# Two chunks share each feed-forward product behind a recurrence, with fewer gate banks, more sum banks and output stores by batch

## The chip, the cores and the metric

The kernel runs on one core of a Trainium2 chip. The metric is the device time of one execution in microseconds. The engines are TensorE (PE in the profile, with its weight loads as PEld), VectorE (DVE), ScalarE (ACT), GpSimd (POOL) and SyncE (SP, which here only issues transfers and reads a flag).

## The reference

An attention-like recurrence over 768 steps (4 batches, 8 heads of 40), then two gated feed-forward layers on the 3072 tokens of 320 features, each with 1536 hidden features:

```python
for t in range(S):
    y[:, :, t] = einsum('bhd,bhde->bhe', r_t, state)
    Sa = einsum('bhde,bhe->bhd', state, a_t)
    state = state * w_t[:, :, None, :] - einsum('bhd,bhe->bhde', Sa, b_t) + einsum('bhd,bhe->bhde', v_t, k_t)
x = y.transpose(0, 2, 1, 3).reshape(3072, 320)
x = (silu(x @ w_gate) * (x @ w_val)) @ w_out          # moe
x = (sigmoid(x @ w2_gate) * (x @ w2_val)) @ w2_out    # moe2
```

## The kernel before

The tokens are cut into 12 chunks of 256. Every f32 product is made from two-part splits: an upper part in fp32r and the rest, with three products for each pair. So a hidden block `f` (128 of the 1536 features, 12 blocks) of a chunk takes 16 matmuls of 256 columns for gate and value (`Ffn.gate`, line 1109: eight each; `w[..]` weights stationary, the chunk's `x` moving), a silu or sigmoid on ScalarE (1113), a multiply on VectorE (1114), the split of the product into `hh` (ScalarE, 1115) and `hl` (GpSimd, 1116), and 6 matmuls of 320 columns that add the block to two sums `po0`, `po1` (`Ffn.add`, 1125). The adds of block `f` come behind the products of block `f+1`.

The first part of the program (`attention`, called from line 1348) makes the recurrence chunk by chunk and weaves into it the weight decode of layer 1 and layer-1 blocks of chunks that are ready (there gate and value share one bank, `gv`). How many blocks each chunk got there stands in `used`: 3, 5, 5, 5, 5, 5, 5, 5, 5, 7, 10 and 12. All of its feeds `x` are kept in DRAM (`xd`), the partial sums in `xs`.

The second part, from line 1351 on, is the stream (`Ffn.stream`, 1143): a list of jobs, one for each chunk and layer. The 11 chunks with layer-1 blocks left come first (72 blocks), then layer 2 for all 12 chunks (144 blocks): 216 chunk-steps of 16 products and 6 adds. Layer-1 jobs load `x` from `xd` (`load_x`), and their sums are added to `part` on VectorE (`end1`, 1401) and stored. Layer-2 jobs load that result, transpose and split it (`split_x`, `split_steps`, 1055), and copy their two sums on ScalarE and VectorE (`end2`, 1409), then store them (1410), each as one transfer of 2 x 64 x 320, since the two halves of the 128 partitions belong to two batches. Gate and value have two banks each (`g0`, `g1`, pool `b_pg` with 2 buffers).

Layer-2 weights come as pairs of 32-bit words of 64-bit floats and are decoded in 36 steps of 384 or 320 columns (`load_w`, three steps for each of 12 blocks). A step is: absolute value into `dt` on ScalarE (1005); clamp on GpSimd (1008); shift (1011) and merge (1012) on VectorE; sign and exponent into `ds` (1016, 1017) on VectorE; upper part `w` on ScalarE (1027); rest on GpSimd (1029) and its sum with `ds` into `w` (1031 and 1033, or 1035). In the stream the work tiles `dt` and `ds` come from two places in turn (`m_tmp` and `at_static`), and two weight buffers (`m_wb`) are spare, so that decoding starts before layer-1 weights come free. `each1` calls up to three decode steps a layer-1 job, then all that are left.

A scheduler sets the order of instructions on each engine from these calls and from the tiles they wait for; within an engine that order is then fixed. Behind the stream, line 1446 reads a flag and 1447 branches over a fallback that doesn't run on these inputs:

```python
ok = nc.values_load(fl[0:1, 0:1], min_val=0, max_val=1)
with tc.If(ok < 1):
```

Of the kernel before, what the change touches and what calls it, by code (L numbers as in the profile page):

```python
# [18 lines left out]
P = 128  # L19
# [5 lines left out]
FEW = 3  # L25
NWB = 2
DM = H * D
# [8 lines left out]
def raw_of(pool, tags=RAW):  # L36
    return [(pool, t) for t in tags]
# [940 lines left out]
class Ffn:  # L978
# [64 lines left out]

    def split_steps(self, xs):

        nc = self.nc
        x = self.new_x()
        lo, hi = slice(0, 64), slice(64, 128)
# [80 lines left out]
    def ffn(self, x, ws, silu, tag):  # L1129
# [11 lines left out]
        self.used = f  # L1141

    def stream(self, jobs):

        pend = None
        get = jobs[0][3]
        for j, (ws, silu, tag, _, each, end) in enumerate(jobs):  # L1150
            for x in get:
                pass
            get = iter(()) if j + 1 == len(jobs) else jobs[j + 1][3]
            ops = self.sums(tag)
            for f, w in enumerate(ws):
                h = self.gate(x, w, silu)
                if pend is not None:
                    pend()
                last = f == len(ws) - 1

                def pend(ops=ops, w=w, h=h, f=f, last=last, end=end):
                    self.add(ops, w, h, f == 0, last)
                    if last:
                        end(ops)

                each(f)
                if f >= len(ws) - 4 and (nx := next(get, None)) is not None:
                    get = iter((nx,))
        pend()
# [116 lines left out]
def rwkv_moe_kernel(ctx, tc, r, k, v, w, a, b, aw0, aw, aa, akb, av, avt, art, w1a, w2a, out):  # L1286
# [11 lines left out]
    with ExitStack() as c1:  # L1298
# [52 lines left out]
        with ExitStack() as c2:  # L1351
            pool2 = lambda n, b, **kw: c2.enter_context(tc.tile_pool(name=n, bufs=b, **kw))
            wb = pool2("m_wb", NWB)
            y_p, x_q = pool2("m_y", 2), pool2("m_xq", 1)
            pt, pg, po = pool2("b_tp", 2, space=PSUM), pool2("b_pg", 2, space=PSUM), pool2("b_po", 1, space=PSUM)

            tmp = pool2("m_tmp", 1)
            raws = [[t, *raw_of((st, tmp)[i % 2])[1:]] for i, t in enumerate(three)]
            ffn = Ffn(nc, ident, (raws, x_p, h_p, pt, pg, po), False)
            slots = [(wb, "w8")] * NWB + [(st, t) for t in spare_tags] + first + [(st, t) for t in tags]  # L1360

# [4 lines left out]

            ahead = load_w2()

            left = [blk for blk in range(NB) if used[blk] < NF]

            def load_x(blk):
                ffn.x = (x_q, x_p)[left.index(blk) % 2]
                x = ffn.new_x()
                nc.sync.dma_start(out=x.bitcast(F32), in_=xd[blk])
                yield x

            def split_x(blk):
                xin = y_p.tile([P, 2, DM + 64], F32, tag="xin", name="xin")
                src = xs[1][2 * blk : 2 * blk + 2].rearrange("u p e -> p u e")
                nc.sync.dma_start(out=xin[:, :, 0:DM], in_=src)  # L1380
                nc.sync.dma_start(out=xin[:, :, DM:], in_=src[:, :, 256:DM])
                yield
                ffn.x = (x_q, x_p)[(len(left) + blk) % 2]
                yield from ffn.split_steps([xin[:, 0], xin[:, 1]])

            parts = {}

            def each1(blk, f):
                if f == 0:
# [8 lines left out]
            def end1(blk, ops):  # L1398
# [7 lines left out]
            def end2(blk, ops):  # L1406
# [5 lines left out]
            def check(blk, f):  # L1412

                if f in (2, 6, 10):
# [23 lines left out]
            flag, jobs, seen = [], [], []  # L1438
            for blk in left:
                jobs.append((w1[used[blk] :], True, "po", load_x(blk), partial(each1, blk), partial(end1, blk)))  # L1440
            for blk in range(NB):
                jobs.append((w2, False, "po", split_x(blk), partial(check, blk), partial(end2, blk)))
            ffn.stream(jobs)
# [54 lines left out]
```

## Time and profile before

| | us |
|---|---|
| median of 3 runs | 1301.01 (1299.7 to 1302.88) |
| the profiled execution, own time | 1302.28 |
| its span in the trace | 1300.6 |
| TensorE, VectorE, ScalarE, GpSimd busy | 1204.2, 710.7, 600.4, 561.7 |
| 0 to 600: TensorE busy | 524.9 |
| 600 to 675: TensorE busy | 67.3 |
| 675 to 850: TensorE busy | 174.3 |
| 850 to 1288.5: TensorE busy | 437.7 |
| 1288.5 to 1300.6: TensorE busy | 0.0 |

The lower rows cut the span by what is done: recurrence, its last chunk with layer-1 blocks, the stream while the second layer's weights are decoded, the stream after that, and what follows TensorE's last matmul. Matmuls overlap in the records (a `g` of 256 columns has a mean duration of 282 ns), so the time that one takes is read from the starts of neighbours, not from that mean. The granted clock is TensorE's, as a share of 2.4 GHz; its mean over the span is 0.948.

### The profile page before, as it was taken

To read this page: it belongs to the slowest core of one execution; us is meant where nothing else is said; L and a number is where in the kernel's file an instruction comes from. 1 tells how busy PE (TensorE), PEld (TensorE's weight loads), DVE (VectorE), ACT (ScalarE), POOL (GpSimd) and SP (SyncE) were. 2 spreads that over 40 slices of the span, in tenths; PEclk is the share of its full clock that TensorE was granted. 3 is DMA by queue.
4 is the path that set the end of the run, shared out by engine and by line. 5 is a ranking of instruction groups with operands and counts; after the bars stand their busy time and mean duration, and the time that the engine had idled before them with its cause. 6 is when DMAs were issued, how large, how long until landed. Compare 5 with 4: busy or idle time off the path is not lost.

```text
span 1300.6 us, 34364 instructions
## 1 busy us (share of the span) xinstructions
PE 1204.2 (93%) x14209; PEld 1158.9 (89%) x14209; DVE 710.7 (55%) x1432; ACT 600.4 (46%) x1447; POOL 561.7 (43%) x749
## 2 busy tenths in 40 slices
PE   5477989999999999899989999999999999999996
PEld 4466878889889998898889999999999999999996
DVE  6858558876788667966889877322111212121121
ACT  8354555656655665455434444323333333333331
POOL 5767143323223324357867898422222222222221
PEclk8677767999999999999999999999999999999998
DMA  7445534545644554333555544211000000000000
GB/s 216 128 126 150 157 113 116 132 95 130 158 112 107 112 145 119 93 102 112 177 181 162 179 140 143 88 63 42 11 23 23 24 23 23 24 23 23 11 11 14
DMA packets 179750, 124.56 MB, mean 96 GB/s; under 512 B 133888, under 2 KB 159488, under 8 KB 178816
## 3 DMA queue, kind: packets, MB, share of 16 engines
q1 hardware_dynamic: 179584, 122.27, 34.1%
q8 instruction: 113, 1.85, 0.6%
q14 instruction: 53, 0.43, 0.1%
HBM read 90.81 MB, written 31.43 MB: 94 GB/s over the span
## 4 chain that ended last, share of the span: by engine, by line
PE 59%; DVE 19%; ACT 8%; issue 5%; DMA 4%; POOL 3%; SPq 0%; POOLq 0%; ACTq 0%; DVEq 0%
PE g L1109 32%; PE po L1125 16%; DVE pr L525 4%; PE gv L1109 2%; DVE part L531 2%; PE kps L485 2%; PE aps L858 1%; PE tp L370 1%; DVE lq L497 1%; DMA wt<-in_a_w_dram 1%; ACT bn L495 1%; DVE g L1114 1%; DVE am L867 1%; DVE part L822 1%; ACT bn L494 1%
## 5 line engine op out<-in xcount | busy, mean ns | idle before, releaser
L1109 PE MATMUL g<-x,w 128*128 128x256 f32 x3456 | 478.6, 282 | 3.3 <-DVE g L1114 2.6
L1109 PEld LDWEIGHTS g<-x,w 128*128 128x128 f32 x3456 | 449.7, 190 | 4.0 <-DVE g L1114 3.1
L1116 POOL TENSOR_TENSOR hl<-g,hh 128x256 fp32r<-128x256 f32 x288 | 224.9, 782 | 462.8 <-ACT hh L1115 452.7
L1114 DVE TENSOR_TENSOR g<-g,g 128x256 f32<-128x256 f32 x216 | 91.2, 423 | 357.0 <-PE g L1109 347.2
L1115 ACT CAST hh<-g 128x256 fp32r<-128x256 f32 x288 | 116.8, 406 | 247.3 <-DVE g L1114 221.8
L1125 PE MATMUL po<-w,hh 128*128 128x320 f32 x1152 | 227.2, 311 | 1.8 <-ACT hh L1115 1.6
L1125 PEld LDWEIGHTS po<-w,hh 128*128 128x128 f32 x1152 | 176.4, 189 | 2.8 <-ACT hh L1115 2.7
L1109 PE MATMUL gv<-x,w 128*128 128x256 f32 x1152 | 167.8, 294 | 5.3 <-DVE g L1114 3.2
L1109 PEld LDWEIGHTS gv<-x,w 128*128 128x128 f32 x1152 | 149.9, 195 | 8.5 <-DVE g L1114 4.4
L1125 PE MATMUL po<-w,hl 128*128 128x320 f32 x576 | 143.5, 314 | 3.1 <-POOL hl L1116 3.0
L1113 ACT ACTIVATE g<-g 128x256 f32<-128x256 f32 x216 | 82.7, 383 | 125.9 <-PE g L1109 118.3
L1029 POOL TENSOR_TENSOR dt<-dt,w 128x384 f32<-128x384 f32 (+1 forms) x72 | 79.0, 1098 | 72.8 <-ACT w L1027 39.2
L1125 PEld LDWEIGHTS po<-w,hl 128*128 128x128 f32 x576 | 93.1, 189 | 4.9 <-POOL hl L1116 4.7
L497 DVE TENSOR_TENSOR lq<-kps,part 64x256 f32<-64x256 f32 x96 | 40.5, 422 | 77.1 <-ACT bn L495 72.0
L525 DVE TENSOR_TENSOR pr<-part,sn 128x4 f32<-128x4 f32 (+4 forms) x135 | 75.3, 558 | 3.7
L485 PE MATMUL kps<-lq,kbt 104*128 104x128 f32 x384 | 62.4, 312 | 11.5 <-DVE lq L497 8.6
L485 PEld LDWEIGHTS kps<-lq,kbt 104*128 104x128 f32 x384 | 54.5, 219 | 15.8 <-issue 4.4
L531 DVE TENSOR_REDUCE part<-pr 128x2 f32<-128x4 f32 (+4 forms) x135 | 66.6, 493 | 2.9
L1011 DVE TENSOR_SCALAR dt<-dt 128x384 int32<-128x384 int32 (+1 forms) x72 | 48.7, 677 | 30.5 <-POOL dt L1008 30.3
L1027 ACT CAST w<-dt 128x384 fp32r<-128x384 f32 (+1 forms) x72 | 35.6, 495 | 58.6 <-DVE dt L1012 57.1
L858 PE MATMUL aps<-rbd,ut 104*128 104x128 f32 x384 | 57.1, 295 | 4.6 <-DVE ysb L903 2.0
L370 PE MATMUL tp<-ident,part 128*104 128x128 f32 x288 | 46.0, 297 | 15.3 <-ACT pend L178 6.3
(182 smaller groups left out, 1650.3 us busy)
## 6 DMA issues: line engine op xcount, KB each, us to landing
raw<-in_w_dram SPq DMA_DIRECT2D x48, 384.0 KB
xd<-x SPq DMA_DIRECT2D x12, 896.0 KB
x<-xd SPq DMA_DIRECT2D x11, 896.0 KB
raw<-in_w_dram SPq DMA_DIRECT2D x24, 320.0 KB
ld<-in_a_kb_dram SPq DMA_DIRECT2D x22, 320.0 KB
ld<-rd SPq DMA_DIRECT2D x64, 80.0 KB
pn<-pd SPq DMA_DIRECT2D x32, 160.0 KB
ld<-in_a_a_dram SPq DMA_DIRECT2D x12, 320.0 KB
```

The source lines that it names most:

```text
L370: t = nc.tensor.transpose(ps[0 : x.shape[1], n, :], x, ident)
L485: nc.tensor.matmul(kps[:, n].rearrange("p h t -> p (h t)"), lhsT=kbt[0:PW, n, :], rhs=lq[m % 3][0:PW, 4 * g4 + n].rearrange("p h t -> p (h ...
L525: nc.vector.tensor_tensor(out=o, in0=xs[:, 0:kk, None, 0:n].to_broadcast([P, kk, 2, n]), in1=sn[:, None, n : n + 2, 0:n].to_broadcast([P, ...
L531: nc.vector.tensor_reduce(out=xs[:, 0:kk, n : n + 2], in_=o, axis=AX.X, op=ALU.add)
L858: nc.tensor.matmul(aps[:, n, h2], lhsT=ut[0:PW, x, 2 * h2 : 2 * h2 + 2].rearrange("p u s -> p (u s)"), rhs=rbd[0:PW, x, h2].rearrange("p b ...
L1029: sub(out=tf, in0=tf, in1=w.bitcast(F32), op=ALU.subtract)
L1109: nc.tensor.matmul(gv[n], lhsT=p, rhs=q, start=e == 0, stop=e == len(seq) - 1)
L1113: nc.scalar.activation(out=g, in_=gv[0], func=AF.Silu if silu else AF.Sigmoid)
L1114: nc.vector.tensor_tensor(out=g, in0=gv[1], in1=g, op=ALU.mult)
L1115: nc.scalar.copy(out=hh, in_=g)
L1116: self.heng.tensor_tensor(out=hl, in0=g, in1=hh.bitcast(F32), op=ALU.subtract)
L1125: self.nc.tensor.matmul(ops[u], lhsT=p[:, us], rhs=q, start=first and n == 0, stop=last and n == 2)
```

## The change

`Ffn.gates` takes the place of `Ffn.gate` in the stream. A feed tile `x` holds two chunks ([P, 2, XW]), a matmul's moving operand is [2, 256], 512 columns, and a bank holds both chunks' products ([P, 2, 256]). So gate and value have one bank each (`b_pg` with 1 buffer), and the sums have four (`po00`, `po01`, `po10`, `po11`). Jobs are pairs of chunks: (0, 1) to (8, 9) and 10 alone in layer 1, six pairs in layer 2. Where the two chunks of a job differ in `used`, the first blocks are made for one chunk alone, and the last block of the last job is made chunk by chunk. Counted by blocks, 33 pairs and 6 singles make up layer 1, 71 pairs and 2 singles layer 2. The silu, multiply, `hh` and `hl` stay one instruction for each chunk.

`m_wb` and `m_tmp` are gone: all layer-2 steps use one `dt` and one `ds`, and the last two weights go into slots of layer-1 weights (`late`). `each1` calls one decode step for each pair block, two for late weights. The feed pool has two pair buffers (`m_xq`). `end2` stores each sum in two transfers of 64 x 320, one for each batch, on ScalarE's queue for `u == 0` of the last chunk. Line numbers below 1040 shift by -1 (the decode is 1004 to 1034, its VectorE lines 1010, 1011, 1015, 1016), the stream's products are line 1163, silu 1167, multiply 1170, `hh` 1171, `hl` 1172, adds 1124.

The diff, cut to its core:

```diff
+    def gates(self, x, w, silu, act):
+        wh, wl = w
+        n = len(act)
+        cols = lambda at: x[:, act[0] : act[0] + n, at : at + 256]
+        gv = [self.pg.tile([P, 2, 256], F32, tag=f"g{k}", name=f"g{k}") for k in range(2)]
+        for k in range(2):
...
+            for e, (p, at) in enumerate(seq):
+                nc.tensor.matmul(gv[k][:, 0:n], lhsT=p, rhs=cols(at), start=e == 0, stop=e == len(seq) - 1)
...
+        for j in range(n):
+            nc.scalar.activation(out=g[j], in_=gv[0][:, j], func=AF.Silu if silu else AF.Sigmoid)
+        for j in range(n):
+            hh, hl = new("hh", F32R), new("hl", F32R)
+            nc.vector.tensor_tensor(out=g[j], in0=gv[1][:, j], in1=g[j], op=ALU.mult)
+            nc.scalar.copy(out=hh, in_=g[j])
+            self.heng.tensor_tensor(out=hl, in0=g[j], in1=hh.bitcast(F32), op=ALU.subtract)
...
     def stream(self, jobs):
...
-            ops = self.sums(tag)
-            for f, w in enumerate(ws):
-                h = self.gate(x, w, silu)
-                if pend is not None:
-                    pend()
+            ops = [self.sums(f"po{i}") for i in range(len(firsts))]
+            for f in range(min(firsts), len(ws)):
+                act = [i for i, n in enumerate(firsts) if n <= f]
                 last = f == len(ws) - 1
...
+                for part in [[i] for i in act] if last and j + 1 == len(jobs) else [act]:
+                    hs = self.gates(x, ws[f], silu, part)
+                    if pend is not None:
+                        pend()
...
-            wb = pool2("m_wb", NWB)
-            y_p, x_q = pool2("m_y", 2), pool2("m_xq", 1)
-            pt, pg, po = pool2("b_tp", 2, space=PSUM), pool2("b_pg", 2, space=PSUM), pool2("b_po", 1, space=PSUM)
-            tmp = pool2("m_tmp", 1)
-            raws = [[t, *raw_of((st, tmp)[i % 2])[1:]] for i, t in enumerate(three)]
+            y_p, x_q = pool2("m_y", 2), pool2("m_xq", 2)
+            pt, pg, po = pool2("b_tp", 2, space=PSUM), pool2("b_pg", 1, space=PSUM), pool2("b_po", 1, space=PSUM)
+            raws = [[t, *raw_of(st)[1:]] for t in three]
...
-            slots = [(wb, "w8")] * NWB + [(st, t) for t in spare_tags] + first + [(st, t) for t in tags]
+            slots = [(st, t) for t in spare_tags] + first + [(st, t) for t in tags]
...
-                if 1 <= f <= 3:
-                    next(ahead, None)
-                if blk == left[-1] and f == NF - 1 - used[blk]:
+                if i + 1 < len(blks) and used[blks[i + 1]] <= f:
+                    return
+                rest = pairs[pairs.index(blks) + 1 :]
+                for n in range(1 if len(w2) < late else 2):
+                    at = len(w2) - late + NFA
+                    if len(w2) < late or (f > at and all(used[b] > at for p in rest for b in p)):
+                        next(ahead, None)
+                if not rest and f == NF - 1:
                     for _ in ahead:
                         pass
...
                 for u in range(2):
                     (nc.scalar.copy, nc.vector.tensor_copy)[u](out=ob[:, u], in_=ops[u])
-                    nc.sync.dma_start(out=out_rows(out, 2 * blk + u), in_=ob[:, u])
+                    eng = nc.scalar if blk == NB - 1 and u == 0 else nc.sync
+                    rows = out_rows(out, 2 * blk + u)
+                    for b2 in range(2):
+                        eng.dma_start(out=rows[b2], in_=ob[64 * b2 : 64 * b2 + 64, u])
```

TensorE's order in layer 1 of the stream, before. A `g` is a bank (gate or value) of one chunk and block, `w_...` the weights of a block, `po_...` the sums; `x6` stands for six such instructions in a row:

```order
L1109 MATMUL g_9954<-x,w_9194 128x256 x7
L1125 MATMUL po_9695<-w_8527,hh 128x320 x2
L1125 MATMUL po_9696<-w_8527,hh 128x320 x2
L1109 MATMUL g_9954<-x,w_9194 128x256
L1109 MATMUL g_9955<-x,w_9194 128x256 x8
L1125 MATMUL po_9695<-w_8527,hl 128x320
L1125 MATMUL po_9696<-w_8527,hl 128x320
```

And now:

```order
L1163 MATMUL g_9896<-x,w_8485 128x512 x8
L1163 MATMUL g_9897<-x,w_8485 128x512 x8
L1124 MATMUL po_9690<-w_7833,hh 128x320 x2
L1124 MATMUL po_9691<-w_7833,hh 128x320 x2
L1124 MATMUL po_9692<-w_7833,hh 128x320 x2
L1124 MATMUL po_9693<-w_7833,hh 128x320 x2
L1124 MATMUL po_9690<-w_7833,hl 128x320
L1124 MATMUL po_9691<-w_7833,hl 128x320
L1124 MATMUL po_9692<-w_7833,hl 128x320
L1124 MATMUL po_9693<-w_7833,hl 128x320
```

Sixteen products of both chunks now stand in a row, and the twelve adds of the block before stand behind all of them, no longer between them.

VectorE in the same part of the stream, before. Lines 1011 to 1017 are one decode step, 1114 the multiply of a block:

```order
L1114 TENSOR_TENSOR g<-g_9924,g 128x256
L1011 TENSOR_SCALAR dt<-dt 128x384
L1012 SCALAR_TENSOR_TENSOR dt<-raw,dt 128x384
L1114 TENSOR_TENSOR g<-g_9955,g 128x256
L1016 TENSOR_SCALAR ds<-dt 128x384
L1017 SCALAR_TENSOR_TENSOR ds<-raw,ds 128x384
L1114 TENSOR_TENSOR g<-g_9986,g 128x256
```

And now (1010 to 1016 are the step, 1170 the multiply):

```order
L1170 TENSOR_TENSOR g<-g_10012,g 128x256 x2
L1010 TENSOR_SCALAR dt<-dt 128x320
L1011 SCALAR_TENSOR_TENSOR dt<-raw,dt 128x320
L1015 TENSOR_SCALAR ds<-dt 128x320
L1016 SCALAR_TENSOR_TENSOR ds<-raw,ds 128x320
L1170 TENSOR_TENSOR g<-g_10071,g 128x256 x2
```

The multiplies of both chunks come together, and a whole decode step lies between one pair's and the next.

TensorE where chunk 11's last layer-1 blocks (`gv`) are made. Before, no product of the stream stands among them:

```order
L1109 MATMUL gv<-x,w_7791 128x256 x9
L1125 MATMUL po_9283<-w_2028,hh 128x320 x2
L1125 MATMUL po_9284<-w_2028,hh 128x320 x2
L1109 MATMUL gv<-x,w_7791 128x256 x5
L1125 MATMUL po_9283<-w_2028,hl 128x320
L1125 MATMUL po_9284<-w_2028,hl 128x320
```

And now (line 1163 is the stream's first block, of chunk 0 alone):

```order
L1163 MATMUL g_9694<-x,w_2028 128x256 x3
L1108 MATMUL gv<-x,w_7791 128x256 x4
L1124 MATMUL po_9283<-w_2028,hh 128x320 x2
L1124 MATMUL po_9284<-w_2028,hh 128x320 x2
L1108 MATMUL gv<-x,w_7791 128x256 x3
L1124 MATMUL po_9283<-w_2028,hl 128x320
L1124 MATMUL po_9284<-w_2028,hl 128x320
L1108 MATMUL gv<-x,w_7791 128x256 x9
L1163 MATMUL g_9694<-x,w_2028 128x256 x3
```

The stream's first products now stand in small groups between those blocks.

## Rows read from the trace of the kernel before

**Rows 1.** Table by stretch: us, length, busy time (records) of each engine, granted clock, DMA.

```profile
700.00:750.00 50.00, 49.50 (x393) 49.30 (x392) 41.67 (x68) 22.96 (x59) 43.68 (x57) 1.00 0.53 177
1000.00:1250.00 250.00, 250.00 (x1988) 249.97 (x1988) 49.72 (x113) 82.68 (x212) 69.20 (x102) 1.00 0.07 20
```

**Rows 2.** Page, costliest groups: gate products of the stream; busy, mean ns of one, idle before.

```profile
L1109 PE MATMUL g<-x,w 128*128 128x256 f32 x3456 | 478.6, 282 | 3.3 <-DVE g L1114 2.6
```

**Rows 3.** Timeline of two steps, layer 2: start us, us, engine, instruction, [idle before <-releaser].

```profile
1200.29 0.38 ACT L1113 ACTIVATE g<-g 128x256 f32<-128x256 f32 x1 [0.66 <-PE g L1109]
1200.32 1.81 PE L1109 MATMUL g<-x,w 128*128 128x256 f32 x14
1201.53 0.42 DVE L1114 TENSOR_TENSOR g<-g,g 128x256 f32<-128x256 f32 x1 [2.35 <-PE g L1109]
...
1201.97 0.74 PE L1125 MATMUL po<-w,hh 128*128 128x320 f32 x4
1201.99 0.41 ACT L1115 CAST hh<-g 128x256 fp32r<-128x256 f32 x1 [1.32 <-DVE g L1114]
...
1202.47 0.74 POOL L1116 TENSOR_TENSOR hl<-g,hh 128x256 fp32r<-128x256 f32 x1 [2.03 <-ACT hh L1115]
...
1205.85 1.81 PE L1109 MATMUL g<-x,w 128*128 128x256 f32 x14
```

**Rows 4.** Groups by form, 640 to 820 us: the decode; busy us, mean ns, idle before, releasers.

```profile
L1029 POOL TENSOR_TENSOR dt<-dt,w 128x384 f32<-128x384 f32 x24 | 28.3, 1181 | 10.7 <-DVE ds L1016 8.7 <-ACT g L1113 1.3 <-ACT dt L1005 0.6
...
L1012 DVE SCALAR_TENSOR_TENSOR dt<-raw,dt 128x384 int32<-128x384 int32 x24 | 20.9, 869 | 0.6
...
L1031 POOL TENSOR_TENSOR w<-dt,ds 128x256 fp32r<-128x256 f32 x24 | 19.3, 803 | 0.8 <-DVE ds L1017 0.8
L1011 DVE TENSOR_SCALAR dt<-dt 128x384 int32<-128x384 int32 x24 | 18.1, 752 | 2.2 <-POOL dt L1008 2.0
...
L1008 POOL TENSOR_SCALAR dt<-dt 128x384 f32<-128x384 f32 x24 | 14.6, 610 | 0.7 <-ACT dt L1005 0.7
L1033 POOL TENSOR_TENSOR w<-dt,ds 64x128 fp32r<-64x128 f32 x23 | 12.9, 563 | 0.9
L1005 ACT ACTIVATE dt<-raw 128x384 f32<-128x384 f32 x23 | 12.7, 553 | 4.5 <-POOL w L1035 3.8 <-POOL w L1033 0.7
L1027 ACT CAST w<-dt 128x384 fp32r<-128x384 f32 x24 | 12.3, 513 | 20.6 <-DVE dt L1012 20.6
```

**Rows 5.** Decode lines, whole run: engine, operation, count: shortest/median/longest ns, first and last start.

```profile
L1011 DVE TENSOR_SCALAR dt<-dt x72: 308/702/2207, 21.9 to 819.4; 128x384 int32<-128x384 int32 x48, 128x320 int32<-128x320 int32 x24
...
L1012 DVE SCALAR_TENSOR_TENSOR dt<-raw,dt x72: 475/660/1428, 22.9 to 820.3; 128x384 int32<-128x384 int32 x48, 128x320 int32<-128x320 int32 x24
...
L1029 POOL TENSOR_TENSOR dt<-dt,w x72: 857/1026/1586, 25.1 to 822.1; 128x384 f32<-128x384 f32 x48, 128x320 f32<-128x320 f32 x24
```

**Rows 6.** TensorE's timeline at the start of the stream.

```profile
675.20 4.45 PE L1109 MATMUL g<-x,w 128*128 128x256 f32 x24 [2.14 <-DVE g L1114]
679.45 0.67 PE L1125 MATMUL po<-w,hl 128*128 128x320 f32 x2
```

**Rows 7.** Timeline of the end: ScalarE's last copy and SP's last stores.

```profile
1288.40 0.42 ACT L1409 COPY ob<-po 128x320 f32<-128x320 f32 x1 [1.32 <-PE po L1125]
...
1288.85 1.12 SPq L1410 DMA_DIRECT2D out_dram<-ob  x2
```

**Rows 8.** The branch behind the stream (line 1447), as SP's queue has it.

```profile
L1447 SPq EVENT_SEMAPHORE  x8: 17/17/17, 1293.0 to 1298.8; - x8
...
L1447 SPq COMPARE_BRANCH  x1: 50/50/50, 1290.0 to 1290.0; - x1
```

**Rows 9.** Table by stretch: three microseconds: the stream's start, 128x320 stores, behind the last copies.

```profile
677.00:678.00 1.00, 1.00 (x7) 1.00 (x7) 0.42 (x1) 0.37 (x1) 1.00 (x1) 0.50 0.08 28
883.00:884.00 1.00, 0.92 (x8) 0.68 (x7) 0.20 (x1) 1.00 (x1) 0.00 (x0) 1.00 0.89 310
1291.00:1292.00 1.00, 0.00 (x0) 0.00 (x0) 0.00 (x0) 0.00 (x0) 0.00 (x0) 0.50 0.20 47
```

More of the change, by code (lines that the diff above doesn't have):

```diff
@@ L25 @@
 FEW = 3
-NWB = 2
 DM = H * D
@@ L1149, in stream @@
         get = jobs[0][3]
-        for j, (ws, silu, tag, _, each, end) in enumerate(jobs):
+        for j, (ws, silu, firsts, _, each, end) in enumerate(jobs):
             for x in get:
@@ L1153, in stream, with pend @@
             get = iter(()) if j + 1 == len(jobs) else jobs[j + 1][3]
-            ops = self.sums(tag)
-            for f, w in enumerate(ws):
-                h = self.gate(x, w, silu)
-                if pend is not None:
-                    pend()
-                last = f == len(ws) - 1
[L1161 to L1167, printed above, removed]
+            ops = [self.sums(f"po{i}") for i in range(len(firsts))]
+            for f in range(min(firsts), len(ws)):
+                act = [i for i, n in enumerate(firsts) if n <= f]
+                last = f == len(ws) - 1
+                for part in [[i] for i in act] if last and j + 1 == len(jobs) else [act]:
+                    hs = self.gates(x, ws[f], silu, part)
+                    if pend is not None:
+                        pend()
+                    def pend(ops=ops, w=ws[f], hs=hs, f=f, part=part, last=last, end=end, firsts=firsts):
+                        for i, h in zip(part, hs):
+                            self.add(ops[i], w, h, f == firsts[i], last)
+                            if last:
+                                end(i, ops[i])
+                for i in act:
+                    each(i, f)
+                if f >= len(ws) - 7 and (nx := next(get, None)) is not None:
                     get = iter((nx,))
@@ L1365, in load_w2 @@
                     w2.append(ffn.w)
-            ahead = load_w2()
+            ahead, late = load_w2(), len(spare_tags) + NFA
             left = [blk for blk in range(NB) if used[blk] < NF]
[L1371 to L1374, printed above, removed]
-                yield x
[L1377 to L1381, printed above, removed]
-                yield
-                ffn.x = (x_q, x_p)[(len(left) + blk) % 2]
-                yield from ffn.split_steps([xin[:, 0], xin[:, 1]])
+            twos = lambda xs: [xs[i : i + 2] for i in range(0, len(xs), 2)]
@@ new lines, in rwkv_moe_kernel, with new_x, load_x, split_x @@
+            pairs = twos(left)
+            def new_x():
+                return x_q.tile([P, 2, XW], F32R, tag="x", name="x")
+            def load_x(blks):
+                x = new_x()
+                for i, blk in enumerate(blks):
+                    nc.sync.dma_start(out=x[:, i].bitcast(F32), in_=xd[blk])
+                yield x
+            def split_x(blks):
+                xins = []
+                for blk in blks:
+                    xin = y_p.tile([P, 2, DM + 64], F32, tag="xin", name="xin")
+                    src = xs[1][2 * blk : 2 * blk + 2].rearrange("u p e -> p u e")
+                    nc.sync.dma_start(out=xin[:, :, 0:DM], in_=src)
+                    nc.sync.dma_start(out=xin[:, :, DM:], in_=src[:, :, 256:DM])
+                    xins.append(xin)
+                yield
+                x = new_x()
+                for i, xin in enumerate(xins):
+                    for _ in ffn.split_steps([xin[:, 0], xin[:, 1]], x[:, i]):
+                        yield
+                yield x
@@ L1386, in rwkv_moe_kernel, with each1 @@
             parts = {}
-            def each1(blk, f):
-                if f == 0:
+            def each1(blks, i, f):
+                blk = blks[i]
+                if f == used[blk]:
                     part = parts[blk] = y_p.tile([P, 2, DM], F32, tag="part", name="part")
                     nc.sync.dma_start(out=part, in_=xs[1][2 * blk : 2 * blk + 2].rearrange("u p e -> p u e"))
-                if 1 <= f <= 3:
-                    next(ahead, None)
-                if blk == left[-1] and f == NF - 1 - used[blk]:
+                if i + 1 < len(blks) and used[blks[i + 1]] <= f:
[6 more added lines that the diff above has]
+                if not rest and f == NF - 1:
@@ L1438, in rwkv_moe_kernel @@
             flag, jobs, seen = [], [], []
[L1439 to L1442, printed above, removed]
+            for blks in pairs:
+                firsts = [used[blk] for blk in blks]
+                jobs.append((w1, True, firsts, load_x(blks), partial(each1, blks), partial(end1, blks)))
+            for blks in twos(list(range(NB))):
+                jobs.append((w2, False, [0, 0][: len(blks)], split_x(blks), partial(check, blks), partial(end2, blks)))
             ffn.stream(jobs)
```

32 lines of the change are left out of this document (26 added, 6 removed).

## The prediction

> **What bounds the kernel now.** I read the table of engines by stretch first. From 1000 to 1250 us TensorE is busy all the time at granted clock 1.00, while VectorE is busy for 50 of the 250 us and GpSimd for 69 [rows 1]. So it is in nearly the whole feed-forward stream: the profile page gives its 3456 gate products 479 us of busy time and only 3.3 us of idle time ahead of them [rows 2]. There only fewer or cheaper matmuls, or what lies ahead of the first and behind the last of them, can move the end. From 700 to 750 us TensorE is as full, but there VectorE (41.7 of 50) and GpSimd (43.7) are nearly full too [rows 1]: this is where the second layer's weights are decoded, and where another order of that work can make TensorE wait.
>
> The timeline of a quiet period gives the price of a matmul. 14 gate products of 256 columns take 1.65 us from start to start (1200.32 to 1201.97), 117.9 ns each. Two steps of 16 gates and 6 adds take 5.53 us (1200.32 to 1205.85), 2.765 us each, which leaves 0.879 us for six adds, 146.5 ns for 320 columns [rows 3]. So 64 columns more cost 28.6 ns, 256 of that kind 114.4, and 3.5 ns would be left for the matmul itself. That is less than the reading tells: 10 ns in the 1.65 us move it by 11. A matmul costs its columns and next to nothing beside them.
>
> **The change, part by part.** The sum is made against the profiled execution, 1302.28 us, which is 1.27 us above the median of the runs shown; so 1.3 us go off at the end.
>
> *Paired products.* The 216 chunk-steps of 16 matmuls become 104 pairs (33 in layer 1, 71 in layer 2) and 8 singles: 3456 products of 256 columns become 1664 of 512 and 128 of 256. 1664 matmuls and as many weight loads go, and no column. The adds, 12 for a pair, stay. A product of 512 columns stands nowhere in the trace. One bound is twice 117.9, 235.8 ns, and saves nothing; a loss I exclude, as the same columns are fed with fewer weights. The other takes every gap away: 512 columns at the 2.4 GHz of clock 1.00 are 213.3 ns, 22.5 ns less, 37 us in all. I take 234.3 ns, 1.5 ns less than two, between nothing and the 3.5 ns of the line through the two sizes shown, since two points speak for that line and none for the other end: 1.5 ns by 1664 is **-2.5 us**. A pair then takes 16 x 0.2343 + 12 x 0.1465 = 5.51 us.
>
> The rows put 256 columns at 117.9 ns at clock 1.00 [rows 3]. The Trainium skill ("TensorE: Matmul & The Clock Gate", section "Back-to-back issue gap") gives a warm matmul its columns at 2.4 GHz and 2.5 ns more. That is 109.2 ns for 256 columns, which this trace does not show, and 215.8 ns for 512: by it the sum would be some 33 us lower. It is rival C.
>
> *Single gate banks.* A pair's first product into a bank must wait until ScalarE (gate) or VectorE (value) has read both chunks' halves of the pair before. Meanwhile TensorE has the other bank's eight products (1.87 us) and twelve adds (1.76 us), 3.6 us; two reads take 2 x 0.38 us on ScalarE, 2 x 0.42 on VectorE [rows 3]. Some 2.8 us are left over, so this costs nothing, unless a reader stands behind other work for that long. The decode is the work that could do it.
>
> *The decode with one work tile.* Before, consecutive decode steps had their own `dt` and `ds`, and two could overlap. Now a step's first operation (ScalarE, absolute value) waits until GpSimd has read `dt` for the step before. The loop is the sum along that chain: by the means of the busy stretch 0.553 + 0.610 + 0.752 + 0.869 + 0.513 + 1.181 + 0.803 + 0.563 = 5.84 us [rows 4], and five changes of engine, of 0.04 us (VectorE's end 1201.95 to ScalarE's 1201.99) to 0.07 us (1202.40 to GpSimd's 1202.47) [rows 3], 0.3 together: 6.1 us. With the shortest times of the three that vary most, 0.308, 0.475 and 0.857 [rows 5], it is 5.0 us. VectorE's new order is strict, two multiplies and then four decode operations, so where the loop is longer than a pair's 5.51 us it delays the multiplies pair after pair and, once the 2.8 us of cover are used, TensorE. By the order some 29 of the 36 steps lie in the stream. Bounds: nothing, and (6.1 - 5.5) x 29 = 17 us. A pair now has at most one step beside it in 5.5 us where two chunk-steps had up to one and a half, so the engines are in each other's way less, and the loop should lie between 5.0 and 5.6. I take **+2 us**.
>
> *The start of the stream.* TensorE's first stream product waits 2.14 us for VectorE, to 675.20, and the next 24 take 4.25 us (to 679.45) where 24 x 0.118 is 2.83: it had been idle, the granted clock fell to 0.50 in 677 to 678, and 1.4 us are lost [rows 6, 9]. In the changed order the first stream products stand as filler among chunk 11's last first-layer steps, as their banks are free once the recurrence is over. That fills the wait, and the low clock goes with it. Late next is chunk 11's own chain from silu to the lower half of the product, which still ends in its adds. Bounds: +2 for a wait of the old size elsewhere, -3.5 for both; I take **-2.5 us**, nearer to the removal that the order shows.
>
> *The stores by batch.* ScalarE starts the first of the two last copies at 1288.40, and SP issues the last stores from 1288.85 on, 0.56 us each [rows 7]. It branches at 1290.0, and its next event is at 1293.0, the last at 1298.8 [rows 8], 1.8 us ahead of the end of the span. For those last 5.8 us SP waits for stores. They move slowly: a share of 0.20 of the DMA engines and 47 GB/s in 1291 to 1292, where two stores of the same bytes in the form 128x320 had 0.89 and 310 GB/s in 883 to 884 [rows 9]. So it is the form 2x64x320 that is slow, and 64 x 320, with its 64 rows in front, should go like 128x320: landed well before SP's 1293.0. Late next is SP's own stretch behind the branch, 3.0 us for which the trace shows no releaser; SP has two issues ahead of the branch, as before, and ScalarE the other two, beside VectorE's copy. The end then comes some 0.4 us behind the old 1293.0 for the semaphores that are read there, and 1.9 us: 1295.3 in place of 1300.6, **-5.3 us**. Bounds 0 and -5.8. The other chunks' 22 additional stores cost SP 0.56 us each over 400 us in which nothing waits for it.
>
> *At nothing:* the splits of a pair's feed, as many as before, beside the 66 us of a job's twelve pair steps; and the two late weights, which go into layer-1 slots that come free pairs ahead of their use.
>
> Sum: 1302.28 - 2.5 + 2 - 2.5 - 5.3 = 1294.0 profiled, **1292.7 us** as a median.
>
> **The rivals.**
> *B: a matmul has a real fixed cost, and two chunks now share it.* 117.9 less 106.7 ns (256 columns at 2.4 GHz) is 11 ns; paid once, 512 columns take 225 ns and 11 x 1664 = 18 us go in place of 2.5: 1277. For it: weight loads halve in number. Against it: 320 columns show 146.5 less 133.3, 13 ns, so the excess grows with the columns.
> *C: a feed of 512 columns leaves no gap,* 213 ns: 37 us in place of 2.5, 1258. Against it: neither size shown comes near its columns' time.
> *D: slower. One work tile paces everything.* Place: the stretch of the decode, 700 to 860 us, where the multiplies stand in order behind the decode and a single bank leaves no second one to run ahead into. Price: the upper bound of above, 17 us in place of 2, 1308. It decides from a loop of 6.0 us (0.5 x 29 = 14 in place of 2, 1305). For it: the means of the stretch [rows 4]. Against it: those were made with two steps under way.
> *E: the smaller stores land no sooner,* and the end stays 12 us behind the last product: 1292.7 + 5.3 = 1298.0. For it: four stores in place of two. Against it: the rows of the 128x320 form.
>
> The Trainium skill ("DMA: Bandwidth & Descriptors", section "Rules for kernel authors") says of two transfers to disjoint halves of the partitions not to bother, since they serialize. That speaks for E; no run here shows a pair of halves.
>
> **How the numbers follow.** A measurement of this kernel tells changes of some 0.3%, 3.9 us: faster is below 1297.1, slower above 1304.9. The forecast gets 0.57, with an own range of 1286 to 1299 (the bounds of the start and the tail, and waits of up to 8 us); 0.07 of it lies within 0.3%. B gets 0.15 and C 0.04, both faster; E 0.09, within 0.3%; D 0.15, of it 0.02 within 0.3% and 0.13 slower. So faster 0.50 + 0.15 + 0.04 = 0.69, same 0.07 + 0.09 + 0.02 = 0.18, slower 0.13. The range, 1274 to 1302, takes in the forecast, B and E, and leaves out C and nearly all of D, 0.18.
>
> **What would show it.** Products of 512 columns 234 to 236 ns apart and a pair every 5.5 us (225 ns is B, 213 is C). TensorE still full at 700 to 850 us; waits on VectorE, ScalarE or GpSimd that sum to over 10 us there are D. No 2 us wait and no low clock where the stream begins. A DMA share near 0.9 for a microsecond behind the last copies, and the end of the span some 7 us behind TensorE's last product (12 is E). I am wrong if a layer-2 pair takes under 5.4 us or a layer-1 pair over 5.8 in the mean.

## The result and the profile after

| | before | changed |
|---|---|---|
| median, us (runs on one chip) | 1300.38 (1299.70 to 1302.88) | 1281.54 (1279.69 to 1282.63) |
| ratio, 95% interval | | 0.9846 (0.9831 to 0.986) |
| profiled execution, span, us | 1302.28, 1300.6 | 1282.63, 1280.9 |

The changed kernel takes 18.8 us less, where 8.3 less were forecast: the time is inside the stated range, and the gain is more than twice the one forecast. The rows of the changed kernel that answer to those of before follow. The table by stretch (columns as in [rows 1]), with one microsecond behind the last copies:

```profile
700.00:750.00 50.00, 50.00 (x263) 43.90 (x262) 29.73 (x62) 21.09 (x54) 36.04 (x49) 1.00 0.43 140
1000.00:1250.00 250.00, 250.00 (x1302) 219.07 (x1302) 44.87 (x112) 78.29 (x213) 71.08 (x104) 1.00 0.07 16
1274.00:1275.00 1.00, 0.00 (x0) 0.00 (x0) 0.00 (x0) 0.00 (x0) 0.00 (x0) 1.00 0.90 221
```

TensorE is full as before, and VectorE and GpSimd have fallen from 41.7 and 43.7 us to 29.7 and 36.0 in 700 to 750. The page's group that answers to [rows 2]:

```profile
L1163 PE MATMUL g<-x,w 128*128 128x512 f32 (+1 forms) x1792 | 419.9, 385 | 0.8 <-DVE g L1170 0.7
```

The idle time ahead of the stream's products has gone from 3.3 to 0.8 us. The timeline of a pair in layer 2 (as [rows 3]):

```profile
1199.80 3.37 PE L1163 MATMUL g<-x,w 128*128 128x512 f32 x14
...
1203.00 0.75 PE L1124 MATMUL po<-w,hh 128*128 128x320 f32 x4
```

14 products of 512 columns take 3.20 us from start to start (1199.80 to 1203.00), 228.6 ns each; I had put 234.3. TensorE's timeline from chunk 11's first layer-1 product on (as [rows 6]):

```profile
639.62 1.21 PE L1108 MATMUL gv<-x,w 128*128 128x256 f32 x8 [0.57 <-ACT x L1060]
...
665.56 0.64 PE L1163 MATMUL g<-x,w 128*128 128x256 f32 x4
...
674.94 0.85 PE L1124 MATMUL po<-w,hh 128*128 128x320 f32 x4 [0.36 <-ACT hh L1114]
675.96 0.55 PE L1124 MATMUL po<-w,hl 128*128 128x320 f32 x2 [0.17 <-POOL hl L1115]
676.38 1.20 PE L1163 MATMUL g<-x,w 128*128 128x256 f32 x8
...
678.29 1.19 PE L1163 MATMUL g<-x,w 128*128 128x256 f32 x8
...
698.84 2.08 PE L1163 MATMUL g<-x,w 128*128 128x512 f32 x8 [0.69 <-DVE g L1170]
...
707.93 3.82 PE L1163 MATMUL g<-x,w 128*128 128x512 f32 x16
...
713.35 3.82 PE L1163 MATMUL g<-x,w 128*128 128x512 f32 x16
```

The kernel before has these two waits ahead of the one in [rows 6]:

```profile
662.63 2.18 PE L1109 MATMUL gv<-x,w 128*128 128x256 f32 x16 [0.54 <-DVE g L1114]
...
672.20 0.86 PE L1125 MATMUL po<-w,hh 128*128 128x320 f32 x4 [0.91 <-ACT hh L1115]
```

The stream's products (line 1163, 256 columns) now fill the gaps among chunk 11's blocks. Where there were waits of 0.54, 0.91 and 2.14 us there are two, of 0.36 and 0.17, and a pair takes 5.42 us (707.93 to 713.35) in place of 5.53. One wait on VectorE is left, 0.69 us at 698.84. Two of the decode's groups, 640 to 870 us (as [rows 4]):

```profile
L1028 POOL TENSOR_TENSOR dt<-dt,w 128x384 f32<-128x384 f32 x21 | 25.2, 1201 | 15.5 <-DVE ds L1015 7.8 <-ACT w L1026 7.7
...
L1010 DVE TENSOR_SCALAR dt<-dt 128x384 int32<-128x384 int32 x22 | 11.5, 521 | 16.7 <-POOL dt L1007 16.6
```

With the means of all eight groups of the loop over one tile, the loop sums to 5.2 us (0.552 + 0.518 + 0.521 + 0.715 + 0.513 + 1.201 + 0.745 + 0.458) and 5.5 with the changes of engine, where the rows of before gave 6.1. The end, as timeline and as SP's queue has the branch (as [rows 7, 8]):

```profile
1271.44 4.52 SPq L1464 DMA_DIRECT2D out_dram<-ob  x6
...
1271.96 0.56 PE L1124 MATMUL po<-w,hl 128*128 128x320 f32 x2
1272.42 0.42 ACT L1460 COPY ob<-po 128x320 f32<-128x320 f32 x1 [1.00 <-PE po L1124]
...
1272.87 1.26 ACTq L1464 DMA_DIRECT2D out_dram<-ob  x2
```

```profile
L1502 SPq EVENT_SEMAPHORE  x8: 17/17/17, 1278.9 to 1279.5; - x8
...
L1502 SPq COMPARE_BRANCH  x1: 45/45/45, 1276.0 to 1276.0; - x1
```

SP issues six small stores one behind the other, four of chunk 10 and two of chunk 11, and comes to its branch 3.5 us behind TensorE's last product (1272.52), where before it was 1.5. Of the 5.8 us of waiting for stores nothing is left: 0.90 of the DMA engines are busy in 1274 to 1275, SP's first event after the branch is 2.9 us later, and its last only 0.6 behind that.

Where the 19.7 us between the two spans went, cut at points with the same work done:

| stretch | before | changed | difference |
|---|---|---|---|
| up to chunk 11's first layer-1 product | 637.43 | 639.62 | +2.19 |
| from there to 24 stream products and the first block's upper adds (680.54, 678.29) | 43.11 | 38.67 | -4.44 |
| from there to TensorE's last product (1288.50, 1272.52) | 607.96 | 594.23 | -13.73 |
| from there to the end of the span | 12.10 | 8.38 | -3.72 |

The first row is no part of the change: in the eleven profiles of whole kernels that point lies between 631.7 and 639.6 us. So the runs below are compared from it on, too.

### The profile page after: what moved, and what is told of

Read it like the earlier page. It is cut to its first block, busy times and chain, and to the rows that moved or that the text cites. A ratio compares the mean times of both kernels' runs of the same rounds, so it can differ in the third digit from the quotient of the medians.

```text
span 1280.9 us, 31386 instructions
## 1 busy us (share of the span) xinstructions
PE 1195.3 (93%) x12545; PEld 1080.0 (84%) x12545; DVE 689.2 (54%) x1432; ACT 593.5 (46%) x1447; POOL 554.6 (43%) x749
## 4 chain that ended last, share of the span: by engine, by line
PE 61%; DVE 20%; ACT 8%; DMA 5%; issue 3%; POOL 2%; SPq 1%; DVEq 0%; ACTq 0%; POOLq 0%
PE g L1163 30%; PE po L1124 16%; PE gv L1108 5%; DVE pr L524 4%; DVE part L530 3%; PE kps L484 3%; DMA wt<-in_a_w_dram 2%; PE aps L857 2%; PE tp L369 1%; PE ups L783 1%; DVE lq L496 1%; DVE am L866 1%; ACT bn L494 1%; DVE g L1113 1%; ACT bn L493 1%
## 5 line engine op out<-in xcount | busy, mean ns | idle before, releaser
L1163 PE MATMUL g<-x,w 128*128 128x512 f32 (+1 forms) x1792 | 419.9, 385 | 0.8 <-DVE g L1170 0.7
L1163 PEld LDWEIGHTS g<-x,w 128*128 128x128 f32 x1792 | 323.2, 188 | 61.5 <-PE g L1163 1.1
L1170 DVE TENSOR_TENSOR g<-g,g 128x256 f32<-128x256 f32 x216 | 82.1, 419 | 342.8 <-PE g L1163 340.4
L1124 PE MATMUL po<-w,hh 128*128 128x320 f32 x1152 | 233.7, 311 | 0.5 <-ACT hh L1114 0.4
L1124 PEld LDWEIGHTS po<-w,hh 128*128 128x128 f32 x1152 | 187.1, 188 | 9.6 <-ACT hh L1114 0.8
L1171 ACT CAST hh<-g 128x256 fp32r<-128x256 f32 x216 | 86.9, 406 | 178.4 <-PE po L1124 168.3
L1124 PE MATMUL po<-w,hl 128*128 128x320 f32 x576 | 151.2, 313 | 3.7 <-POOL hl L1115 3.6
L1167 ACT ACTIVATE g<-g 128x256 f32<-128x256 f32 x216 | 72.9, 381 | 149.7 <-PE g L1163 143.2
L1010 DVE TENSOR_SCALAR dt<-dt 128x384 int32<-128x384 int32 (+1 forms) x72 | 40.5, 563 | 53.6 <-POOL dt L1007 53.3
L493 ACT ACTIVATE bn<-kps 32x256 f32<-32x256 f32 x96 | 35.8, 373 | 53.1 <-PE kps L484 40.8
```

What stands on the lines that cost most here:

```text
L1124: self.nc.tensor.matmul(ops[u], lhsT=p[:, us], rhs=q, start=first and n == 0, stop=last and n == 2)
L1163: nc.tensor.matmul(gv[k][:, 0:n], lhsT=p, rhs=cols(at), start=e == 0, stop=e == len(seq) - 1)
L1167: nc.scalar.activation(out=g[j], in_=gv[0][:, j], func=AF.Silu if silu else AF.Sigmoid)
L1170: nc.vector.tensor_tensor(out=g[j], in0=gv[1][:, j], in1=g[j], op=ALU.mult)
L1171: nc.scalar.copy(out=hh, in_=g[j])
```

## The experiments

**1. Two products in place of one.**

```diff
-                nc.tensor.matmul(gv[k][:, 0:n], lhsT=p, rhs=cols(at), ...)
+            for j in range(n):
+                for e, (p, at) in enumerate(seq):
+                    nc.tensor.matmul(gv[k][:, j], lhsT=p, rhs=x[:, act[0] + j, at : at + 256], ...)
```

> The changed kernel with its pairs, banks, order and stores, but each product of 512 columns issued as two of 256 (chunk by chunk, eight and eight): 1664 matmuls and weight loads come back, no column does. Theory (a product of 512 columns is cheaper than two of 256: the trace after has 14 in 3.20 us, 228.6 ns, against twice 117.9): 7.2 ns x 1664 = 12 us slower than the changed kernel, 1293 to 1294 us, ratio to the kernel before 0.994. Rival (the gain is in the order: sixteen products in a row, adds behind them, one bank each): within 2 us of the changed kernel, ratio 0.985.

Measured: ratio 0.9916 (0.9897 to 0.9936), 1289.36 us median. From chunk 11's first product (631.74) to the last (1274.90) it takes 643.2 us; the changed kernel takes 632.9, the kernel before 651.1. Its timeline:

```profile
1200.34 3.93 PE L1164 MATMUL g<-x,w 128*128 128x256 f32 x32
1204.11 0.46 PE L1124 MATMUL po<-w,hh 128*128 128x320 f32 x2
...
1205.86 3.93 PE L1164 MATMUL g<-x,w 128*128 128x256 f32 x32
```

32 products take 3.77 us, 117.8 ns each, and the pair is back at 5.52 us. So 10 of the 18 us on TensorE are the price of the product (12 expected). The other 8 stay without it: 4.7 at the start (38.4 in place of 43.1 to the same point), and some 3.2 behind it, which the rival had right in kind. Part of these is two waits of before, of 1.2 us together, that are one of 0.6. For the rest, the mean start to start of a 256-column product from 900 us on is 117.9 ns here and 118.5 in the kernel before (leaving out the one in a hundred that comes much later): 0.6 ns by 3456, 2 us. Against 117.9, a product of 512 columns (229.8 in the changed kernel) saves 6.0 ns and not 7.2, 10.0 us.

**2. The old stores in the changed kernel.**

```diff
-                    eng = nc.scalar if blk == NB - 1 and u == 0 else nc.sync
-                    rows = out_rows(out, 2 * blk + u)
-                    for b2 in range(2):
-                        eng.dma_start(out=rows[b2], in_=ob[64 * b2 : 64 * b2 + 64, u])
+                    nc.sync.dma_start(out=out_rows(out, 2 * blk + u), in_=ob[:, u])
```

> The changed kernel with the old output stores (2x64x320, all on SP). Theory (the form of the store sets how long SP waits at the end): the end of the span is again 12 us behind TensorE's last product in place of 8.4, +3.7 us, 1285 us, ratio 0.9875. Rival (the end is set by the branch and what follows it, whatever the stores): 8.4 us and 1281.5 us, ratio 0.985.

Measured: 0.9906 (0.9891 to 0.992), 1289.26 us. SP's part of the end, timeline and branch:

```profile
1268.37 6.72 SPq L1461 DMA_DIRECT2D out_dram<-ob  x4
...
1268.89 0.56 PE L1124 MATMUL po<-w,hl 128*128 128x320 f32 x2
```

```profile
L1499 SPq EVENT_SEMAPHORE  x8: 17/17/17, 1277.9 to 1285.3; - x8
...
L1499 SPq COMPARE_BRANCH  x1: 50/50/50, 1275.1 to 1275.1; - x1
```

The end stands 17.6 us behind the last product (1269.45 to 1287.1), not 12.1, while the work up to it takes 632.2 us, as in the changed kernel. Pairing brings four stores to the end where there were two, and in the old form they share the low rate: the DMA share stays at 0.12 to 0.16 in every microsecond from 1274 to 1284, and SP's last event is at 1285.3. The split is worth 9.3 us in this kernel by these two tails, and 7.8 by the ratios (0.9906 against 0.9846), not 3.7.

**3. Gate banks that come free late.**

```diff
-            pt, pg, po = pool2("b_tp", 2, ...), pool2("b_pg", 1, ...), pool2("b_po", 1, ...)
+            pt, po, pg = pool2("b_tp", 2, ...), pool2("b_po", 1, ...), pool2("b_pg", 1, ...)
```

> The changed kernel, but its two gate banks lie on the banks that hold chunk 11's sums, so the stream's first products can't start before those are read. Theory (the early start fills TensorE's wait and keeps its clock up, worth 4.4 us by the two traces): a wait of 2 us or more and a stretch at granted clock 0.5 where the stream begins, +4 to +6 us, 1286 us, ratio 0.9885. Rival (that wait was only moved elsewhere): within 1.5 us of the changed kernel, ratio 0.985.

Measured: 0.9906 (0.9892 to 0.992), 1288.06 us; 641.1 us from chunk 11's first product to the last, 8.2 more than the changed kernel. TensorE's timeline at the start of the stream, and the table by stretch:

```profile
672.81 0.85 PE L1124 MATMUL po<-w,hh 128*128 128x320 f32 x4 [3.36 <-ACT hh L1114]
674.72 0.90 PE L1124 MATMUL po<-w,hl 128*128 128x320 f32 x2 [1.06 <-POOL hl L1115]
678.95 6.53 PE L1163 MATMUL g<-x,w 128*128 128x256 f32 x32 [3.33 <-ACT ob L1379]
```

```profile
675.00:680.00 5.00, 1.67 (x7) 1.26 (x8) 3.10 (x8) 1.34 (x3) 1.26 (x3) 0.50 0.66 208
```

Three waits of 3.36, 1.06 and 3.33 us, and the granted clock at 0.50 in 675 to 680. With the early products the waits are short and the clock stays at 1.00 (670 to 685 in the changed kernel); without them both are back. The 8.2 us are more than the 4 to 6 expected: this start is worse than that of the kernel before, which had one long wait, of 2.14 us. So the run shows what the early start prevents, and not that it is worth 4.4 us.

**4, 7 and 11. The end's issues on other queues.** Chunk 10's stores of `u == 0` go out on ScalarE's queue (4) or on GpSimd's (7, and 11 beside the changed kernel again, 10):

```diff
-                    eng = nc.scalar if blk == NB - 1 and u == 0 else nc.sync
+                    eng = nc.scalar if blk >= NB - 2 and u == 0 else nc.sync                                    # 4
+                    eng = {NB - 1: nc.scalar, NB - 2: nc.gpsimd}.get(blk, nc.sync) if u == 0 else nc.sync       # 7, 11
```

> The changed kernel with chunk 10's stores of u == 0 on ScalarE's queue too: SP issues four stores behind TensorE's last sums in place of six. Theory (SP's issues, 0.75 us each one behind the other, set its branch at 3.5 us behind the last product and so the end): SP's branch 1.2 to 1.5 us earlier, the span's end about 1 us earlier (ScalarE's two additional issues then limit), 1280.5 us, ratio 0.984. Rival (the landing of the last store sets the end): end unchanged, ratio 0.985.

> The changed kernel with chunk 10's stores of u == 0 on GpSimd's queue: SP and ScalarE then issue four and two behind the last sums. Theory (with six stores on SP its branch was late, with four on ScalarE that engine's last event was): the span ends 6.5 to 7 us behind TensorE's last product in place of 8.4 and 7.6, 1280 us, ratio 0.983. Rival (GpSimd is slow at issuing, and is itself the last to come to the end): 8 us or more, ratio 0.9845.

> The changed kernel again, on one chip with the next: ratio to the kernel before 0.985, tail 8.4 us.

> The changed kernel with chunk 10's stores of u == 0 on GpSimd's queue, beside the changed kernel on the same chip. Theory (the tail is 1.3 us shorter, and nothing else differs): 1.3 us below the changed kernel, ratio 0.984. Rival (the 1.8 us between their medians came from the chip and from the recurrence): no difference.

Measured: 0.9834 (0.9821 to 0.9847) and 1279.37 us for 4; 0.9829 (0.9812 to 0.9845) and 1277.78 for 7; on one chip 0.9844 (0.9824 to 0.9864) and 1281.31 for the changed kernel (10), 0.9832 (0.9808 to 0.9855) and 1279.02 for 11. The tails, from TensorE's last product to the end of the span, are 8.4 and 8.1 us (changed, 10), 7.6 (4), 7.1 and 7.2 (7, 11). The branch in 4, and in 7:

```profile
L1502 SPq COMPARE_BRANCH  x1: 45/45/45, 1270.7 to 1270.7; - x1
...
L1502 ACTq EVENT_SEMAPHORE  x1: 17/17/17, 1275.7 to 1275.7; - x1
```

```profile
L1502 SPq EVENT_SEMAPHORE  x8: 17/17/17, 1274.4 to 1275.1; - x8
...
L1502 SPq COMPARE_BRANCH  x1: 45/45/45, 1271.4 to 1271.4; - x1
...
L1502 ACTq EVENT_SEMAPHORE  x1: 17/17/17, 1274.7 to 1274.7; - x1
```

In 4 SP branches 1.7 us behind the last product (1268.96), but ScalarE's copy stood behind its two additional issues, its last two issues take 2.2 us where they took 1.3, and ScalarE's last event, 1275.7, is now the latest. In 7 GpSimd, done by then, takes the two issues. The tail is shorter in every one of these traces, with GpSimd's queue by 0.8 to 1.3 us, which leaves it just above the 6.5 to 7 us expected. But the end of the changed kernel, unaltered, has tails of 8.2 to 9.3 us in experiments 1, 3 and 8. The intervals overlap, too, and the times do not tell these versions from the changed kernel. By its tail, 7 is the quickest that was run.

**6. The stores alone, in the kernel before.** The diff of 2 the other way round, in the old kernel's `end2`.

> The kernel before with nothing but its output stores by batch (u == 0 of the last chunk on ScalarE's queue). Theory (the form of the store sets how long SP waits): here only chunk 11's four small stores stand at the end, so the term of the prediction holds in full: the span ends 6.8 us behind TensorE's last product in place of 12.1, -5.3 us, 1296 us, ratio 0.996. Rival (small stores land no sooner): 12 us, ratio 1.000.

Measured: 0.9972 (0.9958 to 0.9987), 1296.35 us; the tail is 7.9 us (1284.50 to 1292.4).

```profile
L1450 SPq EVENT_SEMAPHORE  x8: 17/17/17, 1290.4 to 1291.0; - x8
...
L1450 SPq COMPARE_BRANCH  x1: 45/45/45, 1286.9 to 1286.9; - x1
...
L1450 ACTq EVENT_SEMAPHORE  x1: 17/17/17, 1291.3 to 1291.3; - x1
```

That is -4.2 us against 12.1, and -3.6 by the ratio. SP waits for no store any more: its eight events behind the branch follow within 0.6 us, where they took 5.8. What is missing of the 5.3 is ahead of them: SP's two issues take 1.8 us where two of the old form took 1.1, so that its branch stands 2.4 us behind the last product and not 1.5, and the stretch from there to its next event takes 3.5 us and not 3.0.

TensorE's instructions stand in the same order here as in the kernel before, one by one, and so this run tells something of the start as well:

```profile
672.60 3.10 PE L1109 MATMUL g<-x,w 128*128 128x256 f32 x24 [2.15 <-DVE g L1114]
675.54 0.45 PE L1125 MATMUL po<-w,hl 128*128 128x320 f32 x2
```

The wait is the same, but the 24 products behind it take 2.94 us and not 4.25, at a granted clock of 1.00 from 670 to 678. The low clock behind this wait is no fixed part of the kernel before. The stretch from chunk 11's first product to the first block's upper adds takes 41.3 us here in place of 43.1; with the early start it is 37.8 to 38.8 in eight profiles.

**8. Two decode tiles again.**

```diff
-            raws = [[t, *raw_of(st)[1:]] for t in three]
+            tmp = pool2("m_tmp", 1)
+            raws = [[t, *raw_of((st, tmp)[i % 2])[1:]] for i, t in enumerate(three)]
```

> The changed kernel with two dt and two ds tiles in turn, as before. Theory (one tile costs next to nothing: TensorE's waits in the decode's stretch of the trace after sum to 0.7 us): within 1.5 us of the changed kernel, if the start of the stream keeps its early products. Rival (the single tile paces the pairs): 3 to 10 us faster.

Measured: 0.9877 (0.9858 to 0.9896), 1284.05 us. From chunk 11's first product to the last it takes 637.0 us, where six profiles of the changed kernel and of versions of its stores have 631.9 to 633.9: neither the same nor faster, but some 4 us slower. The scheduler's order is another one, and TensorE's waits from 645 us on sum to 3.7 us where the changed kernel has 1.2; two of them:

```profile
689.63 0.85 PE L1124 MATMUL po<-w,hh 128*128 128x320 f32 x4 [1.26 <-ACT hh L1171]
...
694.41 3.96 PE L1163 MATMUL g<-x,w 128*128 128x512 f32 x16 [0.90 <-ACT g L1167]
```

So a second tile gave nothing back. That the order alone makes the 4 us was not tried, nor was a second tile with the order kept; what it could give back there is at most the one wait behind the start, 0.69 us in the changed kernel's trace and 1.75 in that of experiment 10.

**5 and 9. The price of a matmul by itself.** Two kernels of chains without other work, which leave the whole computation out. A chain (5 has `m` = 128 throughout, and in two chains the same `p` each time):

```python
p = w8[:, i % 8 * P : i % 8 * P + m]
nc.tensor.matmul(bank[i // 8 % 2][0:m, 0:cols], lhsT=p, rhs=x[:, 0, 0:cols], start=i % 8 == 0, stop=i % 8 == 7)
```

> A kernel of its own: chains of fp32r matmuls of 128, 192, 256, 320, 384 and 512 columns with eight weights in turn, one of [2, 256] columns in two pieces, and two chains (256 and 512) that name the same weights each time; nothing of the reference is computed, the output holds numbers without meaning. Theory (each matmul has a fixed part, which a pair shares): times on a line through 117.9 ns (256) and 228.6 ns (512): 62.5 (128), 90 (192), 145.6 (320), 173 (384). If the fixed part is the change of weights, the chain with the same weights takes some 7 ns less at 256. Rival (the cost goes by columns, 0.46 ns each, and 512 is a special case): 59, 88, 147 and 176 ns.

> A kernel of its own again (nothing of the reference is computed): chains of 256, 128 and 512 columns with 128, 64 or 32 columns of weights. The chains before showed 2.4 GHz and 13.3 ns for 256 columns and more, and a floor of 111.5 ns below. Theory (both are the weight load): with 64 columns of weights the 13.3 ns and the floor shrink by about half, 256 columns to 113 ns, 128 columns to 60 ns. Rival (the 13.3 ns belong to each matmul whatever its weights): 256 columns stay at 120 ns, 128 columns fall to 66.7 ns (53.3 and 13.3) if the floor alone is the weight load, or stay at 111.5 if neither is.

Measured in 5, from start to start: 226.7 ns (512 columns), 173.4 (384), 146.6 (320), 120.0 (256), 111.5 (192 and 128); with the same weights named each time 227.0 and 120.4. In those two chains, too, the trace has a weight load for every matmul, so they do not tell whether the load is the fixed part. Two rows of the timeline (the first holds 96 products of 512 and 192 of 256):

```profile
20.61 44.95 PE L51 MATMUL c<-x,w 128*128 128x512 f32 x288
65.40 21.95 PE L51 MATMUL c2x<-x,w 128*128 128x512 f32 x96
```

96 products of [2, 256] take 21.79 us, 227.0 ns each: two pieces cost nothing. From 256 columns on all four widths are the columns at 2.4 GHz (106.7, 133.3, 160.0, 213.3) and 13.3 or 13.4 ns, so there the theory of a fixed part holds (173 expected for 384, 176 by the rival). Below there is a floor, which neither had. The timeline of 9, each chain from its start to the next one's:

```profile
21.85 15.51 PE L44 MATMUL a<-x,w 128*128 128x256 f32 x128
37.20 14.68 PE L44 MATMUL b<-x,w 128*64 128x256 f32 x128
51.72 14.67 PE L44 MATMUL c<-x,w 128*32 128x256 f32 x128
66.23 14.40 PE L44 MATMUL a<-x,w 128*128 128x128 f32 x128
80.47 7.84 PE L44 MATMUL b<-x,w 128*64 128x128 f32 x128
88.14 7.85 PE L44 MATMUL c<-x,w 128*32 128x128 f32 x128
95.83 22.03 PE L44 MATMUL a<-x,w 128*128 128x512 f32 x96
117.70 22.24 PE L44 MATMUL b<-x,w 128*64 128x512 f32 x96
139.78 15.51 PE L44 MATMUL e<-x,w 128*128 128x256 f32 x128
```

| columns | weights 128 | 64 | 32 |
|---|---|---|---|
| 128 | 111.3 | 59.9 | 60.1 |
| 256 | 119.9 | 113.4 | 113.4 |
| 512 | 227.8 | 230.0 | |

The floor goes with the weights: at 64 columns of them it is gone, and 128 columns cost 53.3 and 6.6 ns. The Trainium skill ("TensorE: Matmul & The Clock Gate", section "LDWEIGHTS (loading the stationary operand)") gives a weight load a time in ns of its columns divided by 1.2, by estimate 106.7 ns for 128; the floor of 111.3 agrees within 5 ns. The fixed part halves with the weights at 256 columns, as the first theory said, but not from 64 to 32, and not at 512 columns. So the fixed part is no simple share of the weight load, and what it is stays open. So does why in the kernels 256 columns take 118.5 and 512 229.8 (means from 900 us on) where the chains show 120.0 and 226.7.

## Why the prediction was wrong

- **Paired products: the step that failed.** I drew a line through two widths, 117.9 ns (256 columns) and 146.5 (320), found 3.5 ns for the matmul itself, and took 1.5 ns of it for each removed product, -2.5 us. Experiment 1 has 10.3 us, 6.2 ns for each of the 1664: the term was a quarter of what it had to be. The reading was not at fault: the means from 900 us on in the kernel before are 118.5 and 147.0 ns, and the line through these leaves some 4 ns, too. It is the line that does not reach to 512 columns: it has some 233 ns there, and the changed kernel takes 229.8. The means of the two kernels, 2 x 118.5 - 229.8 = 7.2 ns, give 12.0 us, of which 2 are the order (experiment 1). The mechanism was rival B, at somewhat over half of its 18 us: a fixed part of each matmul that two chunks share. Against B I had held that the excess over 2.4 GHz "grows with the columns". In the chains it is 13.3 ns at every width from 256 on. In the kernels' means it does grow, 11.8 ns (256), 13.7 (320) and 16.5 (512), and so sharing it is worth less than B's 11; why, stays open. C is out: 226.7 ns alone and 229.8 here, where the gap rule of the Trainium skill ("TensorE: Matmul & The Clock Gate", section "Back-to-back issue gap"), which the page gives for a matmul by itself, comes to 215.8, an estimate (from my 234.3 ns that would have been 31 us, not 33).
- **The start:** the mechanism was right, the size is known only roughly: -4.4 us between the two profiles in place of -2.5, outside the bound of -3.5. I had priced only the last wait and the low clock; the waits ahead of it (0.54 at 662.63, and 0.91 in place of 0.36) went as well. But 1.4 of the 43.1 us of before were a low clock that experiment 6, with the same order, does not show. Against its 41.3 the early start is worth some 3 us.
- **The stores:** -3.7 in place of -5.3. The form was what made SP wait, by experiments 2 and 6, and E is out. But I took the end's stores to be as many as before. Pairing ends two chunks at once, SP issues six, and its branch comes 2 us later; in the kernel before the same edit brings 4.2.
- **One decode tile:** +2 forecast; the idle time ahead of the stream's products is 0.8 us (3.3 before, most of it at the start), so the term came to nothing that can be seen. D is out: the loop is 5.5 us by the rows after, within the 5.0 to 5.6 I put. That the engines are less in each other's way fits these rows and was not tested.
- **Not foreseen:** some 3 us behind the start that experiment 1 keeps without the wide product: 0.6 us of waits, 2 us of 256-column products that follow 0.6 ns closer in the new order, and a rest. Why they follow closer was not tested.

Sum in TensorE's stretch and the tail, by the traces: -4.4 - 13.7 - 3.7 = -21.9 us, and +2.2 for where the recurrence ended; forecast -8.3.

For the stores' form the Trainium skill has a reason ("DMA: Bandwidth & Descriptors", section "Why a DMA increments its semaphore by 16 and not by 1"): the number of engines of a transfer is the largest up to 16 that divides the slowest dimension on both of its sides. By that 2x64x320 has two engines, a share of 0.125, and 64x320 sixteen. The traces agree: 0.90 in the changed kernel, and in the kernel before 0.13, once the stores move by themselves (us, length, busy time, granted clock, DMA share, GB/s):

```profile
1295.00:1296.00 1.00, 0.00 (x0) 0.00 (x0) 0.00 (x0) 0.00 (x0) 0.00 (x0) 0.50 0.13 46
```

The 0.20 that I read [rows 9] also holds packets of instructions on other queues. The advice of the Trainium skill ("DMA: Bandwidth & Descriptors", section "Rules for kernel authors") against two halves, which I had given to E, compares them with one transfer that already has sixteen engines, which the old store had not.

## What to carry to other kernels

The fixed part of a matmul is paid for each instruction: filling a bank with 512 columns was worth some 6 ns a product here. Two neighbouring widths did not tell it, not even by means over hundreds of starts (4 ns), and chains without other work tell too much (2 x 120.0 - 226.7 = 13.3 ns). A price for a width that stands nowhere in the trace wants a run of that width in place, as experiment 1 is, or bounds as wide as B's. When work is paired, count what now ends together: stores, copies and their issues at the end of the program came twice. And give new buffers the memory that comes free first: the same kernel with its gate banks on late banks lost 8 us on TensorE.

## What was not expected of the hardware

- In the chains of experiment 5, a matmul of 256 to 512 columns costs its columns at 2.4 GHz and 13.3 ns, and no width with 128 columns of weights came below 111 ns in the mean.
- In those of experiment 9, with 64 columns of weights 128-column products run at 60 ns, 256-column ones 6.5 ns faster, and 512-column ones no faster.
- SP's stretch from the branch to its next event is 2.7 to 3.5 us in all eleven profiles of whole kernels, whatever was stored. Packets of instructions, of 8 and 16 KB, move in it; whether SP waits for them was not tested.
